# Four FNet/GEGLU layers in split fp32: z^T turned on VectorE and through memory, sums added to x by an accumulating DMA

## The chip, the cores and the metric

The kernel runs on one core of one Trainium2 chip. The metric is the device time in microseconds (us). Before the change three runs gave 1661.48, 1662.34 and 1665.74 us; their median is 1662.34. One more run was taken under the hardware profiler.

## The reference

Four layers act on x, 2048 tokens (S) by 512 features (D), all in float32: mixing, feed-forward, mixing, feed-forward.

```python
def _A_ref(x, dft_seq_re, dft_seq_im, dft_hid_re, dft_hid_im):
    a = jnp.einsum("bsd,ed->bse", x, dft_hid_re)
    b = jnp.einsum("bsd,ed->bse", x, dft_hid_im)
    return jnp.einsum("ts,bse->bte", dft_seq_re, a) - jnp.einsum("ts,bse->bte", dft_seq_im, b)

def _B_ref(x, w_gate, w_up, w_down):            # F = 1792
    return (_gelu(x @ w_gate) * (x @ w_up)) @ w_down

x = A_x
x = x + _A_ref(_layernorm(x), ...)
x = x + _B_ref(_layernorm(x), ...)
x = x + _A_ref(_layernorm(x), ...)
x = x + _B_ref(_layernorm(x), ...)
```

## The kernel before

**Products.** TensorE multiplies float32r values. Each float32 operand v is split into a rounded part hi (a ScalarE copy, line 110) and the rest lo (a VectorE subtraction, line 111); a product is three matmuls, hi·hi, hi·lo and lo·hi (`mm3`, lines 144 to 146). On top of that both kinds of layer use a Winograd scheme of seven block products in place of eight, so VectorE also makes block sums (S1 to S4 of one operand, T1 to T4 of the other).

**Mixing (`mix`, layers 0 and 2).** The output tokens are taken in four blocks b of 512. The normalized rows z (16 tiles of 128 tokens) are the stationary operand and tiles of the sequence matrices `ws` (128 x 512) the moving one. The stages of a block are A11, A12, S2, S3 and A22; each consists of calls of `six`, six matmuls per call. Then `hid_groups` multiplies by the hidden-size matrices `wh` in eight groups of twelve matmuls (EARLY, MID and LATE), and `x_add` (line 165) adds the four resulting PSUM tiles to x: x was loaded by SP into SBUF, VectorE adds (line 135), GpSimd's queue stores the row tile to a DRAM tile of the next layer. In block 3 the order is S2, S3, A22, EARLY, MID, LATE.

**Feed-forward (`geglu`, layers 1 and 3).** The tokens are taken in two passes w of 1024, each in two parts of 512. For each n of 14 the seven products of the gate or up weights with z^T run (`first`, `second`, `up`; 42 matmuls), the activation follows, and six steps behind (`LAG`) the products with the down weights f = 0 to 13 of part 0 are mixed in (`down_steps`, twelve matmuls for each f); the last six of part 0 and the fourteen of part 1 (`down`) come after the loop. z^T, the operand `blocks`, is made by `block_steps(layer, w)`: four norms, then for each of four feature chunks c four 128x128 transposes on TensorE into one PSUM tile (`turned`, line 454), from which copies, differences and splits are taken; the same for the second half of the pass. For w = 0 these steps run in the last block of the mixing before, from S3 on; for w = 1 in part 1 of the pass w = 0.

**Streams and queues.** `items` is the list of all streamed operands in order of use. `take` splits five items ahead (`AHEAD`) and loads four more ahead of that (`RAW`). All loads are issued by SP, in order; stores by GpSimd's queue, in order, beside its small power operations in the norms (line 378). `queue` holds side work as a list of closures; `step()` runs one of them after each `six`, group or `down`. SBUF tiles come from a ring of 102 slots of 128 x 512, handed out first in, first out, PSUM tiles from eight banks. A scheduler with its own estimate of times decides how the program's instructions stand on each engine; each engine then runs its list in order. A DMA's completion is counted on one of eight counters for SP's and eight for GpSimd's, so each DMA waits until the one eight places ahead on its queue has landed.

**Weights.** The down weights are loaded, split and stored as two halves (`down_weight_steps`, line 693) as side work of layer 0. The gate and up weights are loaded, summed, split and stored by `weight_steps(n)` (line 654): n = 0 and 1 in block 3 of layer 0, the others in the pass w = 0 of layer 1 (`making`). Later passes load the stored halves.

**Opening.** `x_ahead` and `load_next` put four x tiles and four `ws` tiles on SP's queue in turn; 16 small matmuls on the identity warm TensorE; `first_norm(0, 0)` makes the first operand.

Of the kernel before, what the change touches and what calls it, by code (L numbers as in the profile page):

```python
# [28 lines left out]
LAG = 6  # L29
EARLY = 2  # L30
# [8 lines left out]
def fnet_geglu(ctx: ExitStack, tc: tile.TileContext, x_in, ws, wh, wgu, wdn, out):  # L39
# [198 lines left out]
    def as_is(v):  # L238
        return (v,)

# [112 lines left out]
    for layer in range(0, 4, 2):  # L353
        mix_items(layer)
        for _ in range(NB // 2):
            items.extend((F32R, halves(wds[f]), lambda *w: w, None) for _ in range(2) for f in range(NF))
# [84 lines left out]
    def block_steps(layer, w):  # L441

        z, t = {}, {}

        def norm(i):
            def run():
                z[i] = normed(layer, w * 2 * NT + i)
            return run

        def turned(c, part):  # L450

            ps = ps8.get()
            for i in range(NT):
                nc.tensor.transpose(ps[:, i * P:(i + 1) * P], z[part * NT + i][:, c * P:(c + 1) * P], ident)  # L454
            if c == ND - 1:
                sb.put(*(z.pop(part * NT + i) for i in range(NT)))
            return ps
# [6 lines left out]
        def first(c):  # L464
            def run():
                ps = turned(c, 0)
                t[f"B{1 + c // 2}1", c % 2] = copied(ps)
                blocks[f"B{1 + c // 2}1", c % 2] = split_slot(ps)
                ps8.put(ps)
            return run  # L470

        def second(c):
            def run():
                ps = turned(c, 1)
                if c < 2:
                    t["B12", c] = copied(ps)
                    t["T1", c] = difference(ps, t["B11", c])
                    sb.put(t.pop(("B11", c)))
                else:
                    c0 = c - 2  # L480
                    t["T2", c0] = difference(ps, t["T1", c0])
                    t["T3", c0] = difference(ps, t["B12", c0])
                    sb.put(t.pop(("B12", c0)))
                    blocks["B22", c0] = split_slot(ps)
                ps8.put(ps)
# [14 lines left out]
        one = [norm(i) for i in range(NT)] + [first(c) for c in range(ND)]  # L500
# [483 lines left out]
```

## Time and profile before

| | us |
|---|---|
| median of three runs | 1662.34 |
| the profiled run | 1666.76 |
| span of the profile, first to last instruction | 1664.9 |

The span is cut into stretches and groups of instructions below. "Busy" of TensorE (PE) is modelled and counts a matmul until its end, so that overlapping matmuls give a busy PE; how many matmuls fall in a stretch tells more. "Idle before" is the time an engine waited ahead of a group, with what ended it. A DMA's "landing" is the time from its issue to its completion. The granted clock of TensorE is 0.998 over the span.

### The profile page before, as it was taken

Reading aid. Unit: us, or ns where it says so; the run is one execution under the profiler, and the core shown is the slowest. Engines: PE = TensorE matmul, PEld = TensorE weight load, DVE = VectorE, ACT = ScalarE, POOL = GpSimd, SP = SyncE. Lnnn points to the kernel's source line nnn. Section 1 sums busy time; section 2 is a strip of 40 time slices with the busy share of each in tenths; the row PEclk is TensorE's granted clock in tenths of the full one; section 3 lists DMA queues with packets and bytes.
Section 4 is the critical chain, followed back from the end, with each engine's and each line's share of the span. In section 5 each row is a group of like instructions: output and inputs, shape, how many; then the busy total and the mean of one; then the engine's idle time right before and its main releaser. Section 6 shows DMA issues by size and latency. Waiting matters only on the chain.

```text
span 1664.9 us, 22527 instructions
## 1 busy us (share of the span) xinstructions
PE 1650.4 (99%) x7296; PEld 1359.2 (82%) x7296; DVE 1190.7 (72%) x2132; ACT 776.2 (47%) x1352; POOL 169.3 (10%) x288
## 2 busy tenths in 40 slices
PE   9999999999999999999999999999999999999999
PEld 6877788888788888888888888888888888888887
DVE  8997978687887765655898785857946556656561
ACT  7744434255565543534663333444635443444440
POOL 3212100021422110000210000000100000100000
PEclk9999999999999999999999999999999999999999
DMA  9788886778766876555665766565695559755551
GB/s 361 247 279 329 306 317 227 253 252 291 273 229 215 292 269 233 172 189 198 216 227 182 240 228 228 168 227 188 225 386 184 171 177 321 259 178 175 186 183 51
DMA packets 200726, 388.46 MB, mean 233 GB/s; under 512 B 23840, under 2 KB 27424, under 8 KB 200608
## 3 DMA queue, kind: packets, MB, share of 16 engines
q1 hardware_dynamic: 183168, 329.86, 59.1%
q0 software_dynamic: 17440, 57.16, 9.1%
q8 instruction: 58, 0.95, 0.2%
q14 instruction: 60, 0.49, 0.1%
HBM read 328.73 MB, written 58.20 MB: 232 GB/s over the span
## 4 chain that ended last, share of the span: by engine, by line
PE 93%; DVE 3%; DMA 2%; issue 1%; ACT 1%; SPq 0%; DVEq 0%; ACTq 0%
PE p L144 31%; PE p L145 30%; PE p L146 30%; DMA s<-wgu 2%; DVE s L111 1%; PE p L551 1%; PE p L454 1%; DVE s L135 1%; DMA s<-ws 1%; DVE s L132 1%; DMA s<-x 0%; DVE s L725 0%; DVE s L739 0%; DVE s L723 0%; ACT s L110 0%
## 5 line engine op out<-in xcount | busy, mean ns | idle before, releaser
L145 PE MATMUL p<-s,s 128*128 128x512 f32 x2368 | 921.7, 390 | 1.9 <-DVE s L111 1.9
L146 PE MATMUL p<-s,s 128*128 128x512 f32 x2368 | 908.6, 390 | 0.0
L144 PE MATMUL p<-s,s 128*128 128x512 f32 x2368 | 901.2, 391 | 7.0 <-DVE s L135 3.9
L110 ACT ACTIVATE s<-s 128x512 fp32r<-128x512 f32 (+1 forms) x758 | 438.0, 617 | 467.6 <-DVE s L132 98.6
L111 DVE TENSOR_TENSOR s<-s,s 128x512 fp32r<-128x512 f32 (+1 forms) x758 | 490.2, 679 | 87.1 <-ACT s L110 64.3
L144 PEld LDWEIGHTS p<-s,s 128*128 128x128 f32 x2368 | 445.0, 188 | 102.9 <-DVE s L135 5.0
L145 PEld LDWEIGHTS p<-s,s 128*128 128x128 f32 x2368 | 445.4, 188 | 95.0 <-DVE s L111 3.1
L146 PEld LDWEIGHTS p<-s,s 128*128 128x128 f32 x2368 | 445.2, 188 | 93.7 <-DVE s L111 0.7
L135 DVE TENSOR_TENSOR s<-s,p 128x512 f32<-128x512 f32 x316 | 213.0, 685 | 188.9 <-PE p L146 140.6
L139 ACT ACTIVATE s<-p 128x512 f32<-128x512 f32 x248 | 145.2, 593 | 187.4 <-PE p L146 171.4
L132 DVE TENSOR_TENSOR s<-s,s 128x512 f32<-128x512 f32 (+1 forms) x290 | 172.4, 608 | 23.4 <-DMA s<-ws 15.4
L722 ACT ACTIVATE s<-s 128x512 f32<-128x512 f32 x112 | 70.4, 630 | 91.7 <-DVE s L135 90.9
L725 DVE SCALAR_TENSOR_TENSOR s<-s,s 128x512 f32<-128x512 f32 x112 | 76.8, 690 | 38.2 <-ACT s L724 37.6
L378 POOL TENSOR_TENSOR rstd<-rstd,power 128x1 f32<-128x1 f32 x64 | 50.8, 803 | 506.7 <-DVE rstd L377 500.8
L723 DVE SCALAR_TENSOR_TENSOR s<-s,s 128x512 f32<-128x512 f32 x112 | 77.0, 690 | 33.5 <-ACT s L722 31.3
L724 ACT ACTIVATE s<-s 128x512 f32<-128x512 f32 x112 | 69.5, 627 | 25.0 <-DVE s L723 24.4
L135 DVE TENSOR_TENSOR s<-s,s 128x512 f32<-128x512 f32 (+1 forms) x78 | 50.1, 645 | 38.5 <-DMA s<-ws 22.1
L169 POOL DMA_DIRECT2D x<-s x48 | 26.1, 543 | 443.8 <-DVE s L135 440.8
L382 ACT ACTIVATE s<-s,shift,rstd 128x512 f32<-128x512 f32 x64 | 50.4, 811 | 36.5 <-DVE shift L380 32.1
L739 DVE SCALAR_TENSOR_TENSOR s<-s,s 128x512 f32<-128x512 f32 x84 | 58.0, 690 | 1.6
L197 POOL DMA_DIRECT2D wb<-s x84 | 45.2, 540 | 121.6 <-ACT s L110 85.1
L373 DVE BATCH_NORM_STATS2 st<-s 128x6 f32<-128x512 f32 x64 | 42.7, 689 | 19.8 <-DMA s<-x 19.8
(32 smaller groups left out, 254.6 us busy)
## 6 DMA issues: line engine op xcount, KB each, us to landing
s<-ws SPq DMA_DIRECT2D x432, 256.0 KB, 4.0
s<-wb SPq DMA_DIRECT2D x294, 256.0 KB, 4.1
s<-wd SPq DMA_DIRECT2D x224, 256.0 KB, 4.3
s<-x SPq DMA_DIRECT2D x126, 256.0 KB, 4.1
s<-wh SPq DMA_DIRECT2D x120, 256.0 KB, 4.8
wb<-s POOLq DMA_DIRECT2D x98, 256.0 KB, 3.5
x<-s POOLq DMA_DIRECT2D x48, 256.0 KB, 4.1
wd<-s POOLq DMA_DIRECT2D x28, 256.0 KB, 4.9
```

Of the source, the lines that this page charges most:

```text
L110: nc.scalar.activation(hi, src, AF.Copy)
L111: nc.vector.tensor_tensor(lo, src, f32(hi), op=ALU.subtract)
L132: nc.vector.tensor_tensor(out, a, b, op=ALU.subtract)
L135: nc.vector.tensor_tensor(out, a, b, op=ALU.add)
L139: nc.scalar.activation(v, src, AF.Copy)
L144: nc.tensor.matmul(ps, ah, bh, start=start, stop=False, skip_group_check=True)
L145: nc.tensor.matmul(ps, ah, bl, start=False, stop=False, skip_group_check=True)
L146: nc.tensor.matmul(ps, al, bh, start=False, stop=stop, skip_group_check=True)
L722: nc.scalar.activation(t, g, AF.Square)
L723: nc.vector.scalar_tensor_tensor(t, t, 1.0 / GELU_C, g, op0=ALU.add, op1=ALU.mult)
L724: nc.scalar.activation(t, t, AF.Tanh, scale=GELU_A * GELU_C)
L725: nc.vector.scalar_tensor_tensor(t, t, 1.0, g, op0=ALU.add, op1=ALU.mult)
```

## The change

- `turned` on TensorE goes. Each norm of `block_steps` now also turns its z tile in 32x32 blocks on VectorE and stores it to a DRAM tile (GpSimd's queue). A new step `fetch(c)` reads it back with eight DMAs on SP's queue, two parts times four quarters of 32 partitions; each DMA gathers 32 x 16 pieces of 32 elements (128 bytes). `first` and `second` work from these SBUF tiles, and two PSUM copies each are left out.
- The norms of a pass are spread over earlier steps: four from S2 of block 2, four from S3 of block 2. For w = 1, the steps are queued ahead of the last six `down` of part 0.
- `x_gather`: ScalarE copies a PSUM tile, and a DMA of GpSimd's queue adds it to x in DRAM. One set of DRAM tiles serves the three inner values of x, filled at the start by 16 copies of x from DRAM to DRAM. It serves all of the mixing layers' sums and twelve row tiles of layer 1; layer 3 and the last part of layer 1 keep `x_add`.
- The down weights are loaded whole and split at their first use in layer 1 (`make_down_first`); `down_weight_steps` goes. Operands that need no split (`whole`) are loaded at most about two items ahead (`NEAR`).
- Gate and up weights n = 0 and 1 are loaded from S2 of block 3, and the load for n + 3 is issued at the start of `up(n)`.

```diff
-    for layer in range(1, 4):
-        for i in range(NS):
-            xs[layer, i] = dram.tile([P, D], F32, name=f"x{layer}_{i}")
+    for i in range(NS):
+        xs[1, i] = xs[2, i] = xs[3, i] = dram.tile([P, D], F32, name=f"x_{i}")
...
+    def x_gather(layer, i, ps):
+
+        t = copied(ps)
+        ps8.put(ps)
+        nc.gpsimd.dma_start(xs[layer + 1, i], t, accum_op=ALU.add)
+        sb.put(t)
...
+            if stream["loaded"] > n + NEAR and items[stream["loaded"]][2] is whole:
+                break
             load_next()
...
+            if items[stream["split"]][2] is whole and stream["split"] > n + NEAR:
+                break
...
+    def make_down_first(f):
+        def run(v):
+            p = plain(v)
+            kept(wds[f], p)
+            return p
+        return run
...
-        z, t = {}, {}
+        zt, t = {}, {}
+        turned = [dram.tile([TB, D], F32, name=f"t{layer}_{w}_{part}") for part in range(2)]
 
         def norm(i):
+
             def run():
-                z[i] = normed(layer, w * 2 * NT + i)
+                z, v = normed(layer, w * 2 * NT + i), sb.get()
+                nc.vector.transpose(v, z)
+                part, n = divmod(i, NT)
+                nc.gpsimd.dma_start(turned[part][n * P:(n + 1) * P], v)
+                sb.put(z, v)
             return run
 
-        def turned(c, part):
-
-            ps = ps8.get()
-            for i in range(NT):
-                nc.tensor.transpose(ps[:, i * P:(i + 1) * P], z[part * NT + i][:, c * P:(c + 1) * P], ident)
-            if c == ND - 1:
-                sb.put(*(z.pop(part * NT + i) for i in range(NT)))
-            return ps
+        def fetch(c):
+
+            def run():
+                for part in range(2):
+                    v = zt[c, part] = sb.get()
+                    for i in range(P // 32):
+                        cols = turned[part][:, c * P + i * 32:c * P + (i + 1) * 32]
+                        to = v[i * 32:(i + 1) * 32]
+                        nc.sync.dma_start(
+                            to.rearrange("p (j t) -> p j t", t=32), cols.rearrange("(j p) t -> p j t", p=32)
+                        )
+            return run
...
-                ps = turned(c, 0)
-                t[f"B{1 + c // 2}1", c % 2] = copied(ps)
-                blocks[f"B{1 + c // 2}1", c % 2] = split_slot(ps)
-                ps8.put(ps)
+                v = t[f"B{1 + c // 2}1", c % 2] = zt.pop((c, 0))
+                blocks[f"B{1 + c // 2}1", c % 2] = split_slot(v)
...
-        one = [norm(i) for i in range(NT)] + [first(c) for c in range(ND)]
-        two = [norm(i) for i in range(NT, 2 * NT)] + [second(c) for c in range(ND)]
+        one = [norm(i) for i in range(2 * NT)]
+        two = [fetch(c) for c in range(ND)] + [first(c) for c in range(ND)] + [second(c) for c in range(ND)]
...
-            if last:
-                xrows = [x_load(layer, b * NT + i) for i in range(NT)]
...
-                    x_add(layer, b * NT + i, xrows[i], ps)
+                    x_gather(layer, b * NT + i, ps)
...
+            if b == NB - 2:
+                norms, others = block_steps(layer + 1, 0)
+                queue.extend([run for norm in norms[:NT] for run in (norm, None)])
+                rest.extend((norms[NT:], others))
             if last and layer == 0:
-                queue.extend(weight_steps(0))
+                opening_weights.update((n, weight_steps(n)) for n in range(2))
+                queue.extend([opening_weights[0][0], None, opening_weights[1][0], None, *opening_weights[0][1]])
...
-    def down_weight_steps(f):
...
+            if n + 3 in making:
+                making[n + 3][0]()
+            if n + 2 in making:
+                queue.extend(making[n + 2][1])
...
-                x_add(layer, (w * 2 + part) * NT + i, xrows.pop(0), acc[part][i], keep)
+                at = (w * 2 + part) * NT + i
+                if layer == 3 or keep:
+                    x_add(layer, at, xrows.pop(0), acc[part][i], keep)
+                else:
+                    x_gather(layer, at, acc[part][i])
...
+        if w == 0:
+            queue.extend(run for part in block_steps(layer, 1) for run in part)
...
-    for run in [run for f in range(NF) for run in down_weight_steps(f)]:
-        queue += [run, None, None]
+    for i in range(NS):
+        queue.append(lambda i=i: nc.gpsimd.dma_start(xs[1, i], xs[0, i]))
```

More of the change, by code (lines that the diff above doesn't have):

```diff
@@ L605, in s3 @@
             if last:
-                queue.extend(block_steps(layer + 1, 0))
+                queue.extend(rest[1])
                 if layer == 0:
-                    queue.extend(weight_steps(1))
+                    queue.extend(opening_weights[1][1])
+            if b == NB - 2:
+                queue.extend([run for norm in rest[0] for run in (norm, None)])
             for second, k in skewed():
@@ L689, in divide @@
             return run
-        return [load, sums] + [divide(i) for i in range(len(pieces))]
-    def down_weight_steps(f):
-        raw = []
-        def load():
-            raw.append(sb.get())
-            with tc.issue_after(stream["last"].ins):
-                nc.sync.dma_start(raw[0], wdn[f])
-        def store():
-            p = plain(raw[0])
-            kept(wds[f], p)
-            sb.put(*p)
-        return [load, store]
+        return load, [sums] + [divide(i) for i in range(len(pieces))]
     def weight_load(n):
@@ L760, in down_steps @@
             sb.put(*hs, *v)
-        making = layer == 1 and w == 0
+        making = {}
+        if layer == 1 and w == 0:
+            making.update((n, weight_steps(n)) for n in range(2, NF))
+            making[2][0]()
         chain, side, c11, u, w4 = {}, {}, {}, {}, {}
@@ L825, in up @@
             sb.put(*wparts.pop(n)["tiles"])
-            if making and n + 3 < NF:
-                queue.extend(weight_steps(n + 3))
-            elif not making and n + 2 < NF:
+            if not making and n + 2 < NF:
                 weight_load(n + 2)
@@ L875, in geglu @@
             weight_load(1)
-            queue.extend(block_steps(layer, 1))
         elif before_mix:
```

40 lines of the change are left out of this document (24 added, 16 removed).

## The prediction

> **What bounds the kernel now.** I read the page first: busy time by engine, then the chain that ended last.
>
> ```profile
> PE 1650.4 (99%) x7296; PEld 1359.2 (82%) x7296; DVE 1190.7 (72%) x2132; ACT 776.2 (47%) x1352; POOL 169.3 (10%) x288
> PE 93%; DVE 3%; DMA 2%; issue 1%; ACT 1%; SPq 0%; DVEq 0%; ACTq 0%
> ```
>
> TensorE sets the time nearly everywhere: it is busy for 1650.4 of 1664.9 us, 14.5 us idle, and 93% of the chain. So the change can gain in two ways, with fewer matmuls or with less of that idle time, and it loses wherever an operand now comes later than TensorE wants it. Next the windows, to see where the idle time lies and how full the DMA engines are. The columns are PE, PEld, DVE, ACT and POOL busy with their counts, the granted clock, the DMA share and GB/s.
>
> ```profile
> core 0: us, PE busy (x) PEld busy (x) DVE busy (x) ACT busy (x) POOL busy (x), PEclk, DMA share, GB/s
> 0.00:50.00 50.00, 48.06 (x190) 35.16 (x191) 41.75 (x118) 40.72 (x72) 16.45 (x25) 1.00 0.99 357
> 80.00:140.00 60.00, 57.48 (x251) 46.61 (x250) 56.61 (x94) 28.20 (x50) 10.80 (x20) 1.00 0.78 270
> 140.00:210.00 70.00, 67.70 (x293) 55.60 (x292) 61.28 (x100) 31.12 (x55) 16.18 (x30) 0.98 0.91 337
> 350.00:430.00 80.00, 78.97 (x365) 65.33 (x364) 65.49 (x136) 42.13 (x75) 18.50 (x33) 1.00 0.82 279
> 430.00:500.00 70.00, 67.12 (x287) 54.58 (x286) 58.43 (x109) 40.80 (x76) 21.48 (x40) 0.98 0.66 236
> 500.00:560.00 60.00, 59.82 (x263) 49.00 (x262) 47.24 (x84) 32.86 (x61) 16.11 (x30) 1.00 0.69 233
> 800.00:1000.00 200.00, 200.00 (x883) 165.38 (x883) 171.10 (x330) 95.60 (x169) 17.36 (x29) 1.00 0.65 217
> ```
>
> The last row is the undisturbed pace: 883 matmuls in 200 us, 0.2265 us each. Idle are 1.9 us at the start, 2.5 and 2.3 us from 80 to 210, 1.0 us around 350 to 430, and 2.9 and 0.2 us from 430 to 560. In the first 50 us the DMA engines are full (0.99).
>
> **The transposes.** Their group and two pieces of the chain:
>
> ```profile
> L454 PE MATMUL p<-ident,s 128*128 128x128 f32 x128 | 17.0, 272 | 0.0
> 615.73 0.87 PE p L454 x8
> 1195.54 1.75 PE p L454 x16
> ```
>
> A matmul's 272 ns overlaps its neighbours; the chain shows the step from one to the next, 1.75/16 = 0.109 us. 128 of them are 14.0 us of TensorE, on the path, since nothing around them was idle. **-14.0 us**, and I see no way to lose this part of it.
>
> **The down weights.** Their loading and splitting lay in the first layer:
>
> ```profile
> L700 SPq DMA_DIRECT2D s<-wdn x14: 327/330/926, 85.4 to 212.1; - x14
> L111 DVE TENSOR_TENSOR s<-s,s 128x512 fp32r<-128x512 f32 x728 | 478.8, 690 | 85.8 <-ACT s L110 63.0 <-PE p L145 6.7 <-PE p L146 5.5
> L110 ACT ACTIVATE s<-s 128x512 fp32r<-128x512 f32 x728 | 427.3, 626 | 459.2 <-PE p L146 95.0 <-DVE s L132 90.4 <-PE p L145 65.7
> ```
>
> 14 x 0.690 = 9.7 us of VectorE leave the stretch of 80 to 210 us, where it is busy for 117.9 of 130 us and TensorE loses 4.8 us. I take half of that back: **-2.5 us** (bounds 0 and -4.8). The same 14 splits and their 28 stores come back in 430 to 560, where VectorE is busy for 105.7 of 130; it rises to 115.4, still below full. The earlier loads of the gate and up weights work against the 3.1 us of idle time there, the new splits for it: 0 (bounds -3.1 and +3).
>
> **The sums by ScalarE and DMA, and VectorE's transposes.**
>
> ```profile
> L135 DVE TENSOR_TENSOR s<-s,p 128x512 f32<-128x512 f32 x316 | 213.0, 685 | 188.9 <-PE p L146 140.6 <-ACT s L139 47.2
> L139 ACT ACTIVATE s<-p 128x512 f32<-128x512 f32 x248 | 145.2, 593 | 187.4 <-PE p L146 171.4 <-PE p L454 10.7 <-DVE s L725 2.2
> L373 DVE BATCH_NORM_STATS2 st<-s 128x6 f32<-128x512 f32 x64 | 42.7, 689 | 19.8 <-DMA s<-x 19.8
> x<-s POOLq DMA_DIRECT2D x48, 256.0 KB, 4.1
> ```
>
> 44 additions of 685 ns leave VectorE, 44 copies of 593 ns come to ScalarE, and 24 copies of transposes leave it. A 32x32 transpose is not in the trace; every VectorE row of 512 elements from SBUF is near 0.69, so 32 of them are 22 us against the 30 us that leave. All of it lies beside matmuls on other PSUM banks: 0. An accumulating DMA is not in the trace either; as a plain store lands in 4.1 us, I bound it by 4 and 8. Its first reader is a norm of the next layer, two or more matmul groups later for the nearest rows, so it costs 0; without that cover SP would stand at that load for up to 4 us, once.
>
> **The opening.** 14 of the 16 DRAM-to-DRAM copies, and the two operations that make the identity, stand ahead of the first norm's power operation on GpSimd's queue; the last two copies stand ahead of the second.
>
> ```profile
> 0.74 0.39 SPq L162 DMA_DIRECT2D s<-x  x1
> 1.19 0.42 SPq L210 DMA_DIRECT2D s<-ws  x1
> 4.58 0.56 POOL L378 TENSOR_TENSOR rstd<-rstd,power 128x1 f32<-128x1 f32 x1 [3.27 <-DVE rstd L377]
> 6.66 0.81 ACT L382 ACTIVATE s<-s,shift,rstd 128x512 f32<-128x512 f32 x1 [4.41 <-DVE shift L380]
> 7.52 1.55 PE L551 MATMUL p<-s,s 128*128 128x512 f32 x3 [0.58 <-ACT s L382]
> 34.62 1.27 POOL L180 DMA_DIRECT2D m<-s  x2 [2.38 <-ACT s L139]
> q1 hardware_dynamic: 183168, 329.86, 59.1%
> q0 software_dynamic: 17440, 57.16, 9.1%
> ```
>
> GpSimd issues two DMAs in 1.27 us, 0.63 each. 0.74 + 14 x 0.63 + 0.5 = 10.1 us for a power operation that ran at 4.58: the first real matmul, at 7.52 now, comes 5.5 us later. The 14th copy also waits until the sixth has landed, 0.74 + 0.5 + 6 x 0.63 + 4.1 = 9.1, which is no later. Besides, q0 spent 0.091 x 16 x 1664.9 / 57.16 = 42.4 engine-us per MB; 4.2 MB of copies take 178, or 11 us of all 16 engines, in a stretch where they are full. So the bounds are 5.5 and 11. From 7.5 us on TensorE is already never idle in this stretch, so the delay isn't made up. I take **+7 us**, near the lower end, since SP's loads run far ahead of TensorE by 50 us.
>
> **The fetches.** This is the large unknown. Each pass now has 32 DMAs of 64 KB in 512 pieces of 128 bytes, on SP, in front of the stream's loads. In the built order of the first pass all 32 start with S3 of block 3, with one `ws` load among them; the next `ws` tile is first used 103 matmuls, 23.3 us, after the first fetch may start (it waits for a tile that TensorE releases there). In the second pass it is 98 matmuls, 22.2 us, from the last norm's store to a `wd` tile behind the 32; in layer 3 about 31 us, and in its second pass the 32 are cut in halves. ScalarE's splits of fetched tiles stand in front of splits of the stream as well, so late fetches stop both. What is p, the time from one fetch to the next?
>
> - Least: SP's two starts above, 1.19 - 0.74 = 0.45; I take 0.46.
> - From the queue rows: q1 took 0.591 x 16 x 1664.9 / 183168 = 86 ns per packet of 1801 bytes on average, q0 139 ns per packet of 3277. The line through them has 36 ns per 1000 bytes and 21 ns for a packet of none, so 26 ns at 128 bytes. 32 such packets for each engine and the last one, 32 x 26 + 21 = 0.85 us.
> - Most: a small packet as slow as q1's average, 33 x 86 ns = 2.8 us.
>
> I take 0.85: it is an estimate from these rows and lies between an issue that is never held up and packets whose size doesn't matter.
>
> ```profile
> s<-ws SPq DMA_DIRECT2D x432, 256.0 KB, 4.0
> ```
>
> Behind the last fetch come a `ws` tile's landing (4.0), a subtraction and a split, some 5 us, and 0.7 for the load among them. First pass: 32p + 5.7 against 23.3. With p = 0.46 that is 20.4, no stall; with 0.85, 32.9, **+9.6**; with 2.8, +72. Second pass: 32p + 4 against 22.2: 0, **+9.0**, +71. Layer 3, first pass, 29p + 6.4 against 31: 0, 0.05, +57; second pass, two bursts of 16p + 4 against some 22: 0, 0, +27; for differences and splits that queue up behind them on VectorE I add **+3** to the middle value. Together 0, **+22** (21.6), +227.
>
> A page speaks to p. The Trainium skill, "DMA: Bandwidth & Descriptors", section Specifications, asks for at least 512 bytes per transfer and says that below it the DMA engine does read-modify-write. No run here has shown it.
>
> **Sum.** -14.0 - 2.5 + 7 + 22 = +12.5 us. The profiled run's 1666.76 becomes 1679.3. It stood 4.4 us above the median of 1662.34; against that median the forecast is **1675 us**.
>
> **Rivals.**
>
> 1. *The fetches are hidden* (faster). If they go at the pace of issue, p = 0.46, the bursts fit in the lead and the sum is -9.5: 1653. For it: the 430 to 560 and 800 to 1000 rows leave a third of the DMA share free, and 64 KB are a quarter of the bytes of a load. Against it: 350 to 430, where the first burst falls, has a share of 0.82 already. It decides where 2(32p) exceeds the two leads by 9.5, that is p = 0.70; below about 0.62 the gain is over 5 us.
> 2. *Each small packet is written twice.* If a destination piece is read and written back, a packet takes two passes, 52 ns, p = 1.7. The stalls are then 36.8 + 36.2 + 24.7 + 9.2 = 107, and the time 1662 - 9.5 + 107 = 1760. For it: nothing in the rows but that no data packet so small was ever moved here. This is what the section Specifications of the Trainium skill's "DMA: Bandwidth & Descriptors" would lead to.
> 3. *The opening is the loss.* p is small, but copies and loads together hold the first operands for the full 11 us and the idle time of 80 to 210 isn't won back: -14 + 11 = -3, about 1659, no change to speak of. For it: the DMA share of 0.99; against it: a copy needs no more than a store did.
>
> **How the numbers follow.** The forecast (p from 0.72 to 1.25, 1663 to 1711) has 0.45; rival 1 0.30; rival 3 0.13; rival 2 0.12. About 0.3%, 5 us, can be told from no change. Faster holds rival 1 (less an edge): 0.28. The same: rival 3 and edges of both neighbours, 0.16. Slower: the rest of the forecast and rival 2, 0.56. The likeliest case's own range is 1663 to 1711; the range that holds 8 in 10 goes from 1650 (rival 1 with the opening at 5.5 and all 4.8 us won back is 1649) to 1712, and leaves rival 2 and some of its like out.
>
> **What would show it.** TensorE's rows lose 128 instructions and line 454's group is gone: if not, the first term falls. The first matmul of 128x512 comes at 13 to 15 us; at 8, the opening is free. In the DMA part, packets under 512 bytes rise by 65,536 and the completions; the fetches' issues stand 0.8 us apart, and their queue share divided by the packets gives the 26 ns. Near 350 to 400 us and 600 us TensorE is idle for 9 to 10 us each, ended by ScalarE or VectorE working on a stream tile or on fetched tiles; with no idle time there, rival 1 holds; with 30 us and more, rival 2. If gathers' landings or the norms' loads end waits of TensorE, I have mislaid a term.

## The result, and the profile after

| | before | after |
|---|---|---|
| median of four runs, us | 1662.91 | 1713.13 (1707.38 to 1714.37) |
| the profiled run, us | 1666.76 | 1707.38 |
| span of the profile, us | 1664.9 | 1705.6 |
| mean granted clock of TensorE | 0.998 | 0.988 |

The changed kernel is slower: 1.0293 times the time before, 95% interval 1.0266 to 1.0320, some 50 us. The forecast was 1675, that is 12.5 us slower, with a range of 1650 to 1712: the loss is four times the forecast one. The profiled run after the change is the quickest of its four, and the one before stood 4 us above its median, so the two traces are 41 us apart and not 50.

The first lines of the changed kernel's page, busy time and chain. Line numbers have moved: the splits are now L111 (ScalarE) and L112 (VectorE), the matmuls L145 to L147, the first product L583, the norm's row statistics L399, the accumulating DMA L179.

```profile
PE 1650.4 (97%) x7168; PEld 1350.5 (79%) x7168; DVE 1179.5 (69%) x2120; ACT 787.4 (46%) x1372; POOL 206.8 (12%) x336
PE 64%; issue 11%; DMA 11%; DVE 9%; SPq 3%; ACT 1%; POOL 1%; DVEq 0%; POOLq 0%; ACTq 0%
```

The 128 transposes are gone (7296 to 7168), yet TensorE's busy time is the same to the tenth. The clock makes up for them: its mean fell from 0.998 to 0.988, 1% of 1650 us or some 16 us, about what the transposes took (14). TensorE's part of the chain fell from 93% to 64%, DMA rose from 2% to 11%. The same stretches as before, in the view by windows (PE, PEld, DVE, ACT and POOL busy with counts, granted clock, DMA share, GB/s):

```profile
0.00:50.00 50.00, 29.50 (x94) 19.06 (x95) 24.81 (x75) 23.01 (x41) 16.29 (x34) 0.80 0.99 361
350.00:430.00 80.00, 75.11 (x313) 59.66 (x312) 69.49 (x119) 42.03 (x75) 14.39 (x24) 0.96 0.91 265
```

In the first 50 us 94 matmuls run instead of 190. From 350 to 430 us 313 run instead of 365, of which 32 were transposes. Two of the sums of what TensorE waited for (in total, times, longest), and the fetches of the second pass:

```profile
PE p L145 <- DMA s<-wd: 4.0, 1, 4.0
PE p L147 <- DMA s<-wb: 3.4, 1, 3.4
...
623.70 25.24 SPq L490 DMA_DIRECT2D s<-t  x32
```

**The opening.** The timeline of the first 27 us, some of its lines (start, duration, engine, line; in brackets the idle time before and what ended it):

```profile
4.76 13.00 SPq L217 DMA_DIRECT2D s<-ws  x7
12.29 0.59 POOL L404 TENSOR_TENSOR rstd<-rstd,power 128x1 f32<-128x1 f32 x1
24.29 1.31 ACT L111 ACTIVATE s<-s 128x512 fp32r<-128x512 f32 x2 [22.06 <-DMA s<-ws]
25.75 0.81 ACT L408 ACTIVATE s<-s,shift,rstd 128x512 f32<-128x512 f32 x1 [0.15 <-DVE shift L406]
26.62 3.78 PE L583 MATMUL p<-s,s 128*128 128x512 f32 x4 [17.11 <-ACT s L408]
...
20.00:30.00 10.00, 3.38 (x5) 1.50 (x5) 5.11 (x18) 4.53 (x8) 1.90 (x3) 0.50 1.05 393
```

The power operation, which I had taken for the bottleneck, ran at 12.29 us, 2 us later than worked out. The first norm's activation, which needs its result, ran only at 25.75 us, for two reasons. Before, this activation came first in ScalarE's list behind a small warm-up (6.66 us, in the prediction's lines); now the scheduler has put two splits of `ws` tiles in front of it. And those tiles were late: SP's seven loads took 13 us to issue, against 4.15 before, while the copies filled the DMA engines. So the first product came at 26.62 us and not at 7.52; how much the order and how much the loads cost isn't separated. The last line, from the windows, shows a further price: after 17 us without work TensorE was granted half its clock, and 3.78 / 4 = 0.945 us went into a matmul, against 1.55 / 3 = 0.517 before.

**The sums and the fetches.** Groups and DMA rows after:

```profile
L179 POOL DMA_DIRECT2D x<-s x44 | 39.5, 1237 | 354.8 <-ACT s L140 354.6
x<-s POOLq DMA_DIRECT2D x48, 256.0 KB, 7.2
378.19 8.29 SPq L490 DMA_DIRECT2D s<-t  x16
369.15 3.02 ACT L111 ACTIVATE s<-s 128x512 fp32r<-128x512 f32 x6 [4.86 <-DMA x<-s]
```

The median landing of the row with the accumulating DMAs (44 of its 48) is 7.2 us, within my bounds of 4 and 8. The fetches of the first pass stand 8.29 / 16 = 0.52 us apart: there p is close to its least value, 0.46. In the second pass it is 25.24 / 32 = 0.79 (above), near the 0.85 of the forecast, and behind the fetches TensorE waits 4.0 us for a `wd` tile; in layer 3's second pass it waits 3.4 us for a `wb` tile. From 640 to 660 and from 1490 to 1510 us, around these two waits, TensorE runs 63 matmuls each time, where its undisturbed pace gives 88. And the last line is a wait that I had not priced at all: ScalarE stops 4.86 us at a split, because the tile that it is to write is still being read by an accumulating DMA.

### The profile page after: what moved, and what is told of

Same layout as the page of the kernel before. It is cut to its first block, busy times and chain, and to the rows that moved or that the text cites. A ratio compares the mean times of both kernels' runs of the same rounds, so it can differ in the third digit from the quotient of the medians.

```text
span 1705.6 us, 22395 instructions
## 1 busy us (share of the span) xinstructions
PE 1650.4 (97%) x7168; PEld 1350.5 (79%) x7168; DVE 1179.5 (69%) x2120; ACT 787.4 (46%) x1372; POOL 206.8 (12%) x336
## 4 chain that ended last, share of the span: by engine, by line
PE 64%; issue 11%; DMA 11%; DVE 9%; SPq 3%; ACT 1%; POOL 1%; DVEq 0%; POOLq 0%; ACTq 0%
PE p L145 21%; PE p L146 21%; PE p L147 21%; DVE s L112 3%; DMA s<-ws 3%; DMA s<-x 3%; SPq L490 2%; DVE s L133 2%; DVE s L136 2%; DMA x<-s 1%; ACT s L111 1%; DMA t<-s 1%; PE p L583 1%; DMA s<-wgu 1%; DMA s<-t 1%
## 5 line engine op out<-in xcount | busy, mean ns | idle before, releaser
L145 PE MATMUL p<-s,s 128*128 128x512 f32 x2368 | 904.3, 392 | 21.2 <-DVE s L136 8.4
L147 PE MATMUL p<-s,s 128*128 128x512 f32 x2368 | 904.3, 391 | 3.4 <-DMA s<-wb 3.4
L111 ACT ACTIVATE s<-s 128x512 fp32r<-128x512 f32 (+1 forms) x782 | 449.6, 617 | 531.5 <-DVE s L133 125.9
L112 DVE TENSOR_TENSOR s<-s,s 128x512 fp32r<-128x512 f32 (+1 forms) x782 | 502.2, 674 | 144.4 <-ACT s L111 110.3
L145 PEld LDWEIGHTS p<-s,s 128*128 128x128 f32 x2368 | 446.7, 189 | 122.9 <-DVE s L136 12.2
L147 PEld LDWEIGHTS p<-s,s 128*128 128x128 f32 x2368 | 446.6, 189 | 97.2 <-DMA s<-wb 3.8
L136 DVE TENSOR_TENSOR s<-s,p 128x512 f32<-128x512 f32 x272 | 182.8, 682 | 147.6 <-PE p L147 120.1
L140 ACT ACTIVATE s<-p 128x512 f32<-128x512 f32 x268 | 155.8, 592 | 141.3 <-PE p L147 136.2
L133 DVE TENSOR_TENSOR s<-s,s 128x512 f32<-128x512 f32 (+1 forms) x314 | 185.6, 609 | 39.3 <-DMA s<-t 19.6
L136 DVE TENSOR_TENSOR s<-s,s 128x512 f32<-128x512 f32 (+1 forms) x78 | 49.7, 640 | 59.2 <-DMA s<-ws 36.9
L179 POOL DMA_DIRECT2D x<-s x44 | 39.5, 1237 | 354.8 <-ACT s L140 354.6
L399 DVE BATCH_NORM_STATS2 st<-s 128x6 f32<-128x512 f32 x64 | 42.8, 686 | 35.0 <-DMA s<-x 34.9
```

The source lines that it names most:

```text
L111: nc.scalar.activation(hi, src, AF.Copy)
L112: nc.vector.tensor_tensor(lo, src, f32(hi), op=ALU.subtract)
L133: nc.vector.tensor_tensor(out, a, b, op=ALU.subtract)
L136: nc.vector.tensor_tensor(out, a, b, op=ALU.add)
L140: nc.scalar.activation(v, src, AF.Copy)
L145: nc.tensor.matmul(ps, ah, bh, start=start, stop=False, skip_group_check=True)
```

## The experiments

Each kernel's ratio is to the kernel before, run on the same chip. In microseconds a ratio is taken of 1665, as the medians of the kernel before went from 1663 to 1667 from one set of runs to the next.

### The copies of x held back

```
+    with tc.issue_after(pool["last"].ins):     # the last power or store on GpSimd's queue
         nc.gpsimd.dma_start(xs[1, i], xs[0, i])
```

> The changed kernel with its 16 copies of x held behind the opening on GpSimd's queue (after the norms' powers and behind the stores of that stage), nothing else moved. Theory, the copies hold the opening (first 128x512 fp32 matmul at 26.62 us against 7.52 before, TensorE at half its clock until 33 us): the whole 21.7 us come back, first such matmul at 7.5 to 8.5 us, about 1691 us. Rival A, as I had put it on record, the copies cost only 7: about 1706. Rival B, the opening is held by the weights' splits that now stand ahead of the first norm on ScalarE, whatever holds them: 1710 to 1713, first matmul still after 20 us. Rival C, 4.2 MB of copies cost the same wherever the DMA engines are busy: the opening is free again, but TensorE idles 10 us or more where the copies now stand (some 60 to 90 us), about 1700.

Measured: 1699.16 us, ratio 1.0203 (1.0180 to 1.0225), 15 us below the changed kernel (theory: 22). From its timeline and its waits and windows around 110 us:

```profile
6.63 0.81 ACT L409 ACTIVATE s<-s,shift,rstd 128x512 f32<-128x512 f32 x1 [4.40 <-DVE shift L407]
7.50 7.13 PE L584 MATMUL p<-s,s 128*128 128x512 f32 x16 [0.35 <-ACT s L409]
...
105.16 3.99 POOL L974 DMA_DIRECT2D x<-x  x8
ACT s L111 <- DMA s<-wh: 9.6, 2, 8.8
PE p L145 <- ACT s L111: 6.4, 1, 6.4
110.00:120.00 10.00, 3.60 (x15) 2.67 (x14) 4.97 (x9) 2.29 (x5) 3.67 (x8) 0.91 0.95 333
```

The opening is as before (7.50 us). Rival B's time is missed, but its mechanism isn't ruled out: with the copies held back the scheduler puts the norm's activation first again (6.63 us), so the trial took away the splits in front of it together with the copies. Rival C's mechanism holds: behind twelve copies issued from 105 us on, ScalarE waits 8.8 us for a `wh` load, TensorE stands 6.4 us and the granted clock falls (0.91). From 100 to 140 us TensorE runs 136 matmuls, against 171 in the kernel with its own sums (below), which has no copies: some 8 us. So part of the copies' price moved rather than went.

### The copies alone, in the kernel before

```
+    for i in range(NS):
+        queue.append(lambda i=i: nc.gpsimd.dma_start(spare[i], xs[0, i]))
```

> The kernel before with 16 copies of x (256 KB each, from one tensor to another) added on GpSimd's queue, where the changed kernel has them; nothing reads them. Theory, they alone hold the opening as in the changed kernel: the first 128x512 fp32 matmul at some 26 us, 21 to 22 us above before, 1685. Rival A, as I had put it on record: it comes at 13 to 15 us, and 7 us are lost, 1671. Rival B, it takes the changed kernel's other orders as well: 1664, first matmul near 8 us.

Measured: 1686.58 us, ratio 1.0119 (1.0105 to 1.0132), that is +20 us (17 to 22). Its timeline:

```profile
23.77 1.31 ACT L110 ACTIVATE s<-s 128x512 fp32r<-128x512 f32 x2 [21.53 <-DMA s<-ws]
...
26.10 3.54 PE L552 MATMUL p<-s,s 128*128 128x512 f32 x4 [16.32 <-ACT s L383]
```

The theory holds: the copies alone make the whole opening, without any of the other edits, and they change ScalarE's order in the same way (the first line).

### The sums as before

```
-    x_gather(layer, b * NT + i, ps)
+    x_add(layer, b * NT + i, xrows[i], ps)     # x rows loaded, a tensor for each layer, no copies
```

> The changed kernel with the sums as before (rows of x loaded, added by VectorE, stored; a tensor for each layer, no copies); norms, transposes by VectorE, fetches and weights as changed. Theory, the accumulating DMAs crowd the norms that follow them (the stretches near 265 to 317 and 1086 to 1115 us, and half of those near 364 to 419 and 1207 to 1257): 21 us less than the kernel with late copies, about 1670 us, and those two stretches lose their pauses. Rival A, the norms are simply too early behind the sums, whoever makes them: within 5 us of the kernel with late copies, about 1688. Rival B, the fetches make all that is left beside the opening: also about 1688, with the pauses where S3 of the last block begins.

Measured: 1678.93 us, ratio 1.0080 (1.0060 to 1.0099), 20 us below the kernel with late copies, as expected in size. But the theory also had the stretch near 265 to 317 us lose its pauses, and one stayed: 153 matmuls from 280 to 320 us, further below. This kernel takes away both the accumulating DMAs and the late copies, whose 8 us near 110 us go with them; so against VectorE's additions the accumulating DMAs cost some 12. The next kernel takes away the adding alone.

### Plain stores where the accumulating DMAs were

```
-        nc.gpsimd.dma_start(xs[layer + 1, i], t, accum_op=ALU.add)
+        nc.gpsimd.dma_start(xs[layer + 1, i], t)
```

> The kernel with late copies, its 44 accumulating DMAs made plain stores: x isn't added to the products of layers 0 to 2, so each such layer's rows are its product alone, less the add. The same instructions, bytes written and waits otherwise. Theory, an accumulating DMA reads as well as writes and takes the DMA engines for twice as long: some 12 us below the kernel with late copies, about 1679. Rival, the order of norms behind the sums costs, not the adding: equal to the kernel with late copies within 3 us, about 1691.

Measured: 1680.52 us, ratio 1.0087 (1.0066 to 1.0107), 19 us below the kernel with late copies (theory: 12; the rival, none). First the kernel with late copies, then the one with plain stores: the DMA rows, and ScalarE's waits for tiles that a store of sums still holds.

```profile
q0 software_dynamic: 23328, 69.75, 13.3%
ACT s L111 <- DMA x<-s: 23.7, 7, 5.4
```

```profile
L179 POOL DMA_DIRECT2D x<-s x44 | 23.8, 543 | 361.6 <-ACT s L140 358.7
q0 software_dynamic: 20512, 69.75, 11.2%
ACT s L111 <- DMA x<-s: 3.5, 5, 1.1
```

The same bytes, in 2816 packets fewer, and 0.133 x 16 x 1695.7 - 0.112 x 16 x 1678.4 = 600 engine-us less for 44 x 0.262 = 11.5 MB. With q0's average of 43 engine-us per MB in the kernel with plain stores these bytes would take 497, so accumulated they took about 1100: 2.2 times as much. The wait for tiles falls from 23.7 to 3.5 us. The copies stand in both kernels and cost the same (134 matmuls here from 100 to 140 us), and the order of norms behind sums is the same, so the rival falls: it is the adding. Whether it costs TensorE by the tiles that are held, by the busier DMA engines or by GpSimd's longer issue (1237 ns against 543) isn't separated.

### Accumulating only in layers 1 and 2

```
+    if layer == 0:
+        x_add(layer, b * NT + i, xrows[i], ps)
+    else:
         x_gather(layer, b * NT + i, ps)
```

> The changed kernel with the sums of layer 0 as before (loaded, added by VectorE, stored), so that no x has to be copied; ScalarE's copies and accumulating DMAs only in layers 1 and 2. Theory: the late copies cost 7.4 us near 112 us and the gathers of layer 0 another 8 or so, so it stands some 15 us below the kernel with late copies, at 1684, and 5 above the kernel with its own sums. Rival A, the gathers of layers 1 and 2 are the dear ones (7.6 us near 1075 to 1105, 7.6 near 1196 to 1250): 1692. Rival B, gathers cost nothing but for the copies: 1679, equal to the kernel with its own sums.

Measured: 1686.39 us, ratio 1.0112 (1.0076 to 1.0149), 15 us below the kernel with late copies and 5 above the one with its own sums, as the theory had it. But its four runs went from 1679 to 1691 us, and its interval overlaps that of the kernel with its own sums (1.0060 to 1.0099): rival B, that the 28 accumulating DMAs which are left cost no more than VectorE's additions, isn't ruled out. Rival A, 1692, lies outside the interval: the copies and layer 0 carry most.

### The weights' part alone, and its two halves

The kernel before with all of the weights' edits, then with the down weights' half alone:

> The kernel before with one part of the change alone: the down weights kept at their first use, and the gate and up weights loaded ahead. Sums, norms and TensorE's transposes as before. Theory, the weights' part gains what the trace shows in its stretches (5.2 us at 80 to 210, 4.5 us near 430 to 490): 9.7 us below the kernel before, about 1653. Rival A, as put on record, 2.5 us: about 1660. Rival B, the gain of those stretches came from the absent transposes and sums: 1662 to 1664, no change.

Measured: 1666.72 us, ratio 1.0011 (1.0002 to 1.0021). Theory and rival A miss: the part as a whole gains nothing. That is rival B's time, but not for its reason, as one half alone does gain:

```
-    for run in [run for f in range(NF) for run in down_weight_steps(f)]:
-        queue += [run, None, None]
+    items.append((F32, (wdn[f],), make_down_first(f), None))     # first use in layer 1
```

> The kernel before with only the down weights moved: loaded and split at their first use in layer 1, and the stream not run more than two items ahead there. Gate and up weights, sums, norms and transposes as before. Theory, the 4.9 us that the stretch of 80 to 226 us gained in the kernel with all weights moved come from this half and are kept, while the losses at 334 to 363 and 413 to 439 us came from the gate and up weights: 5 us below the kernel before, 1658 to 1659. Rival, the splits and stores come back in layer 1 at the same price: 1663 to 1665.

Measured: 1658.69 us, ratio 0.9955 (0.9939 to 0.9971), 7.5 us faster. Windows of the down weights' half alone, and behind them the same stretch of the kernel with all of the weights' edits:

```profile
140.00:210.00 70.00, 70.00 (x311) 57.98 (x310) 58.24 (x95) 27.70 (x49) 8.07 (x15) 1.00 0.77 262
430.00:500.00 70.00, 70.00 (x310) 57.97 (x309) 66.07 (x123) 47.42 (x90) 29.41 (x55) 1.00 0.76 270
340.00:370.00 30.00, 28.15 (x131) 22.89 (x130) 26.68 (x56) 13.94 (x24) 3.53 (x6) 1.00 0.74 240
```

```profile
340.00:370.00 30.00, 26.25 (x108) 20.98 (x106) 25.08 (x53) 14.55 (x26) 4.75 (x6) 0.89 0.62 207
354.50 0.77 PE L145 MATMUL p<-s,s 128*128 128x512 f32 x1 [3.75 <-DVE s L136]
333.38 3.86 DMA x<-s
337.29 4.17 DMA s<-ws
```

The idle time from 140 to 210 and from 430 to 500 us is gone with the down weights alone (311 and 310 matmuls against 293 and 287 before). Bringing the gate and up weights forward then costs 1.0011 - 0.9955 = 0.0056, 9 us: with four more tiles held from S2 of block 3 on, a `ws` load waits for a tile that a store of sums gives back (the last two lines, from the chain that ended last), VectorE works off what has piled up, TensorE stands 3.75 us, and the granted clock of the stretch falls to 0.89. That is 108 matmuls against 131, 5 of the 9 us. The waits are in the trace; that the four tiles make them is an argument, as no run gave the tiles back. This kernel has no fetches and no accumulating DMAs.

### Rows of the spread norms loaded ahead

```
-    queue.extend([run for norm in norms[:NT] for run in (norm, None)])
+    one += [row(i), row(i + 1), row(i + 2), None, norm(i), row(i + 3)]
+    one += [norm(i + 1), None, norm(i + 2), None, norm(i + 3), None]
```

> The kernel with its own sums (no accumulating DMAs, no copies), and each x row of the spread norms loaded four to six steps of TensorE's work ahead of its norm instead of right in front of it. Theory, the spread norms stand in VectorE's queue waiting for rows that were only just asked for (a wait of 2.64 us at 299.86 us, with the addition that TensorE wants behind it): the pauses near 290 to 319 and 1065 to 1092 us go, 10 us less than 1678.9, about 1669 us. Rival A, the DMA engines or the tiles are short there, and the rows come late however early they are asked for: 1677 to 1681, the same. Rival B, the norms aren't what costs, the fetches are: also the same, with the pauses where S3 of the last block begins.

Measured: 1665.17 us, ratio 0.9996 (0.9981 to 1.0012), 14 us below the kernel with its own sums (theory: 10). The edit does a little more than load rows earlier: each group of norms also starts some steps later, and in the second passes the norms no longer stand one right behind the other. What it took away, in the timeline of the kernel with its own sums (SP's load, then VectorE, then TensorE):

```profile
293.45 0.32 SPq L163 DMA_DIRECT2D s<-x  x1
299.86 0.69 DVE L400 BATCH_NORM_STATS2 st<-s 128x6 f32<-128x512 f32 x1 [2.64 <-DMA s<-x]
303.90 0.65 DVE L136 TENSOR_TENSOR s<-s,p 128x512 f32<-128x512 f32 x1
304.60 0.80 PE L145 MATMUL p<-s,s 128*128 128x512 f32 x1 [3.52 <-DVE s L136]
```

A row asked for at 293.45 us holds VectorE at 299.86, and the addition that TensorE waits for stands behind it in the same list. Four windows of each kernel show where the 14 us are, without rows ahead and with them:

```profile
280.00:320.00 40.00, 36.40 (x153) 29.34 (x152) 31.82 (x64) 14.71 (x23) 4.83 (x8) 0.96 0.88 290
840.00:890.00 50.00, 47.31 (x201) 38.21 (x200) 47.94 (x99) 29.51 (x52) 5.43 (x10) 0.97 0.71 225
1060.00:1100.00 40.00, 37.46 (x158) 30.01 (x157) 38.79 (x78) 20.68 (x35) 5.84 (x9) 0.96 0.49 162
1440.00:1490.00 50.00, 46.89 (x199) 38.17 (x199) 27.41 (x44) 17.64 (x31) 2.17 (x4) 0.97 0.95 303
```

```profile
280.00:320.00 40.00, 38.04 (x168) 31.20 (x167) 33.69 (x66) 16.91 (x28) 5.03 (x8) 1.00 0.89 314
840.00:890.00 50.00, 49.61 (x218) 40.43 (x217) 48.83 (x99) 27.64 (x49) 5.96 (x11) 1.00 0.73 235
1060.00:1100.00 40.00, 37.86 (x165) 30.51 (x164) 37.29 (x79) 20.88 (x35) 8.43 (x11) 1.00 0.58 182
1440.00:1490.00 50.00, 48.85 (x215) 39.80 (x214) 34.97 (x56) 24.73 (x43) 2.16 (x4) 1.00 0.92 295
```

15 + 17 + 7 + 16 = 55 more matmuls, 12.5 us at 0.2265 us each, and each of the four reduced clocks is gone. The first and the third, 22 of the 55, lie where spread norms run. In the fourth, the kernel without rows ahead waits 3.1 us for a `wb` tile whose load stands behind sixteen fetches; the edit reaches this pass's norms too, but why the wait went, and why the second window gained, isn't shown.

Nor does the theory's mechanism carry the whole gain. What VectorE's norms wait for rows, in total, without rows ahead and with them:

```profile
DVE st L400 <- DMA s<-x: 30.8, 17, 3.1
DVE st L400 <- DMA s<-x: 27.1, 13, 3.7
```

These waits fell by 3.7 us, the time by 14. In layer 1 the last of the spread norms now runs at 288 us and not at 299.86, ahead of the addition that TensorE wants; so the norms' new places may have won as much as the earlier loads. The trial doesn't separate them.

With accumulating DMAs and late copies in the kernel, the same edit:

> The changed kernel with late copies (1699.2), and the rows of the spread norms loaded ahead; accumulating DMAs everywhere. Theory, two costs that add: norms that wait for rows just asked for (13.8 us in the kernel with its own sums) and accumulating DMAs (20 us): about 1685. Rival A, one cost and not two: the accumulating DMAs make the rows late however early they are asked for, so hardly anything is won: 1696 to 1699. Rival B, the norms' waiting was the way in which the accumulating DMAs cost, and it goes with them: 1670 to 1675.

Measured: 1693.72 us, ratio 1.0157 (1.0141 to 1.0173), 8 us below the kernel with late copies: between theory and rival A. The two costs don't simply add; why isn't shown. VectorE's waits for rows fell from 28.6 to 20.3 us with the edit, ScalarE's for tiles that an accumulating DMA reads only from 23.7 to 21.4.

### The small pieces at the store, and fetches apart

```
-    nc.gpsimd.dma_start(turned[part][n * P:(n + 1) * P], v)
+    for j in range(P // 32):
+        to = turned[part][:, n * P + j * 32:n * P + (j + 1) * 32]
+        nc.gpsimd.dma_start(to.rearrange(...), v[j * 32:(j + 1) * 32].rearrange(...))
```

> The kernel with its own sums, and the 128-byte pieces moved from the fetch to the store: GpSimd stores each transposed tile in 4 DMAs of 512 small pieces, SP fetches 8 whole tiles of 256 KB in a pass instead of 32 DMAs. The same small packets, on the other queue and earlier. Theory A, the 32 issues of some 0.55 us hold up SP's stream behind them (17 us): the pauses of the stretches near 341 to 397, 624 to 651 and 1456 to 1483 shrink, some 9 us below 1678.9, about 1670. Rival A, the fetches were as good as hidden and what is left beside the transposes' gain are norms and weights: 1677 to 1681. Rival B, small packets on GpSimd's queue are slower than on SP's and hold the norms' own rows up: 1690 or more.

Measured: 1694.38 us, ratio 1.0177 (1.0154 to 1.0199), 16 us above the kernel with its own sums, in time as rival B had it. GpSimd's queue, in that kernel's groups:

```profile
L481 POOL DMA_DIRECT2D t<-s x128 | 82.9, 654 | 62.6 <-DVE s L477 50.0
```

128 issues of 654 ns come to GpSimd's list, which also holds the norms' powers. So the trial says that GpSimd is the wrong place for them; it doesn't price the fetches. The kernel of the next trial does.

The kernel with the down weights moved and only the turn added (spread norms with rows ahead, VectorE's transposes, fetches), gate and up weights and sums as before:

> The kernel before with two things moved: the down weights at their first use (1658.7 alone, 0.9955 of before), and VectorE's transposes with spread norms, rows loaded ahead and small fetches in place of TensorE's transposes. Sums and gate and up weights as before. Theory, the turn is worth its 14 us less what the fetch bursts still cost (near 12), so that it gains a little more on the down weights alone, as it did on the weights-only kernel (1665.2 against 1666.7): 1652 to 1657, ratio to before 0.992 to 0.995. Rival A, without the losses of the gate and up weights in the same stretch (334 to 397 us) the bursts are hidden better and nearly the whole 14 us are won: 1645 to 1648. Rival B, fetches and gate and up weights' loads now meet in S3 of the last block: 1660 or more.

Measured: 1658.17 us, ratio 0.9947 (0.9934 to 0.9961), against 0.9955 for the down weights alone: just inside the theory's ratios (0.992 to 0.995), and not to be told from no gain by the turn. The first burst of fetches in its timeline, and the window around it:

```profile
344.62 1.39 SPq L490 DMA_DIRECT2D s<-t  x3
346.60 7.98 SPq L490 DMA_DIRECT2D s<-t  x13
355.22 9.42 SPq L490 DMA_DIRECT2D s<-t  x16
340.00:370.00 30.00, 29.91 (x132) 24.46 (x131) 27.43 (x47) 13.88 (x24) 2.15 (x4) 1.00 0.87 207
```

All 32 fetches lie in this window, and TensorE is idle for 0.09 of 30 us: here the burst is hidden. The pause that stands at this place in the changed kernel stood there too in the kernel that has only the weights' edits, and no fetches. Last, the same with the fetches in four groups:

```
-    two = [fetch(c) for c in range(ND)] + [first(c) for c in range(ND)] + ...
+    two = [fetch(0), None, fetch(1), None, fetch(2), None, first(0), fetch(3), first(1), None, first(2), None, first(3)]
```

> The kernel of the turn alone, with the four groups of eight fetches two steps of TensorE's work apart instead of one behind the other, and the first splits of each group six steps behind its fetches. Theory, a burst of 32 issues at 0.55 us holds SP for 17 us and what stands behind it comes late: apart, they let the stream's loads through, 4 to 8 us below the turn alone. Rival A, the burst has been hidden and the remaining pauses are those of splits and differences that have more to do in the stage: within 2 us of the turn alone. Rival B, with the groups apart the fetched tiles come later and the work behind them is pushed to the end of the block, where it is done at once: slower than the turn alone by 3 us or more.

Measured: 1662.86 us, ratio 0.9977 (0.9966 to 0.9988), 5 us slower than the turn alone, rival B's time. The burst of the first pass was not what was left to gain: from 340 to 370 us 133 matmuls run, against 132. The losses lie in the second passes (156 matmuls against 170 from 600 to 640 us, 163 against 179 from 1400 to 1440); whether for rival B's reason isn't shown.

## Why the prediction was wrong in size, and right in sign by luck

The kernels form a ladder from before to after, each step one or two edits. The steps are differences of ratios, in thousandths and times 1.665 us:

| step | ratio after it | us |
|---|---|---|
| down weights at first use | 0.9955 | -7.5 |
| turn by VectorE and fetches, rows ahead | 0.9947 | -1.3 |
| gate and up weights ahead | 0.9996 | +8.2 |
| rows not ahead, as in the change | 1.0080 | +14.0 |
| accumulating DMAs, and copies late | 1.0203 | +20.5 |
| copies at the start | 1.0293 | +15.0 |

An interval of a ratio is some 0.0014 to 0.0027 wide to each side, so a step is known to 3 to 6 us.

The step that failed is the pricing of the side work. The prediction put the sums at 0 and the spread norms at nothing, as work beside the matmuls, and the opening at 7. The runs show about 12 us for the sums and 20 for the opening, and moving the norms' rows and places won back 14. The term that gave the forecast its sign, 22 us of fetches, is in good part not there. Term by term:

**The transposes, -14.0.** The 128 instructions went, but the best kernel with the turn gains only 1.3 us on the one without, which is less than can be told. Its trace shows where the rest went: against the kernel without the turn it runs 38 matmuls instead of 55 from 300 to 312 us, 156 instead of 178 from 840 to 880 and 71 instead of 90 from 1060 to 1080, together some 13 us of waits and lower clock. No fetches are issued in these three stretches. Spread norms run shortly before the first and in the third; that they are the cause isn't tested, and the second stretch stays open. "I see no way to lose this part of it" was wrong: the instructions went, but their time was lost to later operands.

**The down weights, -2.5.** Right in kind, too small: 7.5. The upper bound, 4.8, counted only the idle time of 80 to 210 us; the 2.9 us of 430 to 500 went as well, and with both the lower clock behind those pauses. Why 430 to 500 gained, where the splits were to come back, isn't shown.

**Gate and up weights, 0 with bounds of 3.** It cost 8 to 9. The step counted VectorE's splits and left out the tiles: the trace shows a load of the stream waiting for a tile that a store gives back.

**The opening, +7 (5.5 to 11).** The trial with copies alone gives 20. The working followed GpSimd's queue, and that was nearly right (12.29 us against 10.1). It took ScalarE's list as it stood, and with the copies the scheduler put two `ws` splits ahead of the first norm, so that the loads, not the power operation, decide. The loads themselves were held up by about as much as the upper bound says: the last of the seven was issued at 17.8 us instead of 8.2. The lower clock behind the pause was left out as well.

**Sums, 0.** The landing lay in the bound, but I asked only who reads the sum, and not who needs the tile that the DMA reads from: ScalarE's waits for such tiles fell from 23.7 to 3.5 us with plain stores. The adding costs 19 us by that trial; against the sums as they were before, the accumulating DMAs cost some 12, as 8 of the ladder's 20.5 are the late copies. The prediction's last sentence, that a wait ended by the sums' landings or the norms' loads would mean a mislaid term, points the right way: the traces show such waits, on ScalarE and VectorE and so one step ahead of TensorE.

**Spread norms, nothing.** Not priced as a step at all, though they were moved, and each issues a load right in front of the instruction that waits for it. Loading the rows earlier and moving the norms won 14 us, 5 of them in the windows where spread norms run (22 x 0.2265), and 8 in the kernel with accumulating DMAs. How the rest was lost stays open: VectorE's waits for rows fell by 3.7 us only.

**The fetches, +22.** In the changed kernel p went from 0.52 in the first pass to 0.79 in the second. With 0.52 the prediction's own formula gives 32 x 0.52 + 5.7 = 22.3 against 23.3 of lead, no stall, where 9.6 were forecast; the window from 340 to 370 us of the kernel with the turn alone shows none. In the second pass, forecast at 9.0, TensorE waits 4.0 us for a `wd` tile behind the fetches; in layer 3's second pass, forecast at 0, 3.4 us for a `wb` tile. With the clock behind them these two places lose some 6 us each, and other edits have a part in it, since the kernel with the turn alone has neither wait. So rival 1 was right for the first pass, and wrong in its time, 1653, because the other costs were missing.

**Rival 2** falls: with 52 ns for a piece p would be 1.7, and no burst came near it. In the first pass 64 KB in 512 pieces of 128 bytes, 32 on each of 16 engines, went at 0.52 us, some 16 ns at most for a piece. The Trainium skill's "DMA: Bandwidth & Descriptors", section Specifications, by which transfers below 512 bytes are read, modified and written, shows no such price here.

So the forecast had the change slower, and it was, but by luck: the fetches were to make it so, and without their 22 us the sum was -9.5. What made it slower were the copies, the accumulating DMAs, the spread norms and the gate and up weights.

**What beats both kernels.** The down weights' half alone (0.9955) and the same with the turn (0.9947) are both faster than the kernel before, and can't be told apart.

## What to carry to other kernels

When a store becomes slower, ask who needs the tile that it reads from, not only who reads what it writes: in a ring of tiles the next loads and splits wait for it. A load that is issued right ahead of its reader puts its latency into that engine's list, and what stands behind it there waits too; price such side work by where it stands. Asking for the rows a few steps earlier and moving the norms won 14 us here, as much as the transposes were worth, though which of the two did it stays open. DMAs that nobody needs soon still take the engines from those that somebody needs now: sixteen copies cost 20 us. They also changed the order in which the scheduler set another engine's list, so after any edit look at which instruction stands first there. And price the clock with each pause: here 1.8 us without work was once followed by 0.57 of the clock.

## What was not expected of the hardware

- A pause of TensorE of 1.8 us can be followed by a lower clock. In the kernel with the turn alone one wait of 1.8 us is followed by 13 matmuls in 4 us; in the kernel with rows ahead a wait of 2.0 us at the same place is followed by 19 (waits, then windows, of each in turn):

```profile
PE p L145 <- DVE s L136: 1.8, 1, 1.8
304.00:308.00 4.00, 4.00 (x13) 3.09 (x12) 3.91 (x7) 1.74 (x3) 0.00 (x0) 0.57 1.05 401
```

```profile
PE p L145 <- DVE s L136: 2.0, 1, 2.0
304.00:308.00 4.00, 4.00 (x19) 3.31 (x18) 3.90 (x8) 2.10 (x4) 0.00 (x0) 1.00 1.04 388
```

  The Trainium skill's "TensorE: Matmul & The Clock Gate", section on the HAM clock gate, gives an idle window of about 3.4 us, free-running, for the fall to half rate. That the same pause is punished once and not the other time agrees with a window that runs freely; that 1.8 us suffice does not agree with a whole idle window.
- An accumulating DMA took the DMA engines 2.2 times as long per byte as a plain store by the estimate above, and 1237 ns of GpSimd to issue against 543.
- Sixteen copies from one DRAM tensor to another, 4.2 MB, issued on GpSimd's queue, held up loads on SP's: the last of seven was issued at 17.8 us instead of 8.2, about as late as the 11 us of DMA time that the prediction had estimated for the copies.
